# A linear-attention block and a gated MLP in one kernel: a new table of orders, with step 5 transposed by DMA

## Chip, core and metric

The program runs on one core of a Trainium2 chip. The metric is the device time of one execution in microseconds (us); lower is better.

## The reference, cut to what matters

Four batches (B = 4), eight heads (H = 8), 768 positions (S), head size 64. The first half is attention with a decay per head, written block by block with a running state; the second half is an MLP with a gate that mixes the positions. All eight heads of a position make the 512 columns that the MLP reads.

```python
for b in range(nb):                      # blocks of 64 positions
    intra = einsum('bhic,bhjc->bhij', qb, kb) * Dmask
    intra = einsum('bhij,bhjd->bhid', intra, vb)
    inter = einsum('bhid,bhde->bhie', qb * lam_pow, kv_state)
    out[:, :, sl] = intra + inter
    kv_state = lam_block * kv_state + einsum('bhsd,bhse->bhde', kb * rev_pow, vb)
h = maximum(x @ w_in, 0); u, v = h[..., :512], h[..., 512:]
v_n = (v - mean(v)) / sqrt(var(v) + 1e-6)
v_s = einsum('ts,bsd->btd', w_spatial, v_n) + b_spatial
out = (u * v_s) @ w_out
```

## The kernel before

The work is cut into 12 **steps** of 256 positions, three for a batch. A step loads `k`, `q` and `v` (512 KB each, `LK`, `LQ`, `LV`, line 193), scales `k` and `q` by the decay powers into bf16 (`KM`, `QM`, line 328, two halves each) and casts `v` (`VC`, line 182). `kc` and `qc`, the scaled tiles, are transposed into `kT` and `qT`. Two ways of doing that are in the code: on TensorE, eight 128x128 transposes for each of the two tiles and a copy out of PSUM (`TK`, `TQ`, line 363; `EK`, `EQ`), or by one DMA for each tile that SyncE issues (`DK`, line 341; `DQ`, line 345).

Then come, on TensorE, products on quarters of the array, 64 rows by 64 columns: the scores (`SC`, line 393), which VectorE multiplies by the causal mask into `a_sb` (`MK`, line 398); the state's update (`KP`, line 422); and the attention's output (`AV`, lines 456 and 465). The output is copied from PSUM into `xT` (`EX`). All that follows uses the whole array: the two halves of the first MLP product (`PV`, line 490, and `PU`, line 541), for each batch eight spatial products (`PW`, line 567) once all six halves of the normalised `v` (`VN`, lines 526 and 529) stand, and the last product (`PO`, line 578; `PH`, line 587, for half of one). A spatial product accumulates onto a bias that is first copied into its PSUM bank (`GP`). Everything that TensorE makes is taken out of PSUM by ScalarE or VectorE: `EV` and `EU` with a ReLU, `GM` with the gate, `EO` into the output tile, which a store (`ST`, line 601) writes. `LN` and `BN`, `RA`, `RD`, `RB` are the small steps of the decay table and of the normalisation.

The weights come in through the same SyncE queue as the inputs, into staging tiles: `WH` (the first MLP matrix, four loads), `WQ` (the spatial matrix, six), `WP` (the last, one of 1024 KB). Casts to bf16 follow on any engine (`CW`, `CX`, `WC`, `WX`). The spatial matrix is then transposed on TensorE (`WT`, line 553). `FL` (line 306) are products of ones by ones whose result nobody reads.

What sets the order is one string, `ORDER`. A token is the name of a piece, its arguments and its engine: `SC.5.0.0.1.T` is the first half of step 5's scores on TensorE into banks 0 and 1, `EV.6.1.3.A` takes bank 3 out on ScalarE. The loop at the end of the function issues the pieces in the string's order; each engine takes its own pieces strictly in that order, and semaphores hold a piece until what it reads is written and what it overwrites is read. PSUM has eight banks: 0 to 6 are named in the tokens, bank 7 keeps the state. Most tiles of a step exist two or three times (`kT`, `qT`, `kc`, `qc`, `a_sb` twice, inputs and `xT` three times).

```python
with tc.manual_schedule():
    for token in ORDER.split():
        name, *args, e = token.split(".")
        ops[name](e, *map(int, args))
```

Of the kernel before, what the change touches and what calls it, by code (L numbers as in the profile page):

```python
# [16 lines left out]
lam.A BR.A tab.0.A LK.0.S LQ.0.S LV.0.S LQ.1.S LK.1.S LK.2.S LV.1.S LQ.2.S WH.0.S WH.1.S posk.P idn.P msk.P one.D  # L17
row.D FL.1.512.1.1.T FL.1.512.2.1.T FL.1.512.3.1.T LB.6.T FL.1.512.5.1.T FL.1.512.4.1.T FL.1.512.1.1.T FL.1.512.2.1.T
FL.1.512.3.1.T FL.1.512.4.1.T FL.1.512.1.1.T FL.1.512.5.1.T FL.1.512.2.1.T LN.6.A LL.D mkc.D LX.A QM.0.0.P TQ.0.0.1.T
KM.0.0.D KM.0.1.D QM.0.1.P TK.0.0.0.T TK.0.1.4.T TQ.0.1.3.T EK.0.0.0.D QM.1.0.D QM.1.1.D EQ.0.0.1.A EK.0.1.4.A VC.0.P  # L20
SC.0.0.0.1.T EQ.0.1.3.A BB.1.2.T KP.0.6.T BB.0.3.T BE.1.2.A BE.0.3.A SC.0.1.4.5.T TQ.1.0.2.T TQ.1.1.3.T KM.1.1.P
KM.1.0.P MK.0.0.0.1.D KM.2.1.P KM.2.0.P VD.1.1.P TK.1.1.0.T EQ.1.0.2.A SX.0.A EK.1.1.0.A VD.1.0.A MK.0.1.4.5.D
EQ.1.1.3.D TK.1.0.1.T SC.1.1.2.3.T eps.D SY.0.6.D EK.1.0.1.D MK.1.1.2.3.D QM.2.1.P CW.0.P CW.1.P AV.0.0.6.1.T
SC.1.0.4.5.T TK.2.1.0.T TK.2.0.2.T FN.0.6.1.A SA.0.1.D AV.0.1.6.1.T KP.1.3.T EK.2.0.2.A EX.0.0.6.A MK.1.0.4.5.D
AV.1.0.2.6.T QM.2.0.D TQ.2.1.5.T TQ.2.0.4.T FN.1.2.6.A EX.0.1.1.A SA.1.0.D EK.2.1.0.D AV.1.1.2.6.T EQ.2.0.4.A
EQ.2.1.5.D SY.1.3.D CW.2.D CW.3.D EX.1.1.6.A EX.1.0.2.A SC.2.1.0.1.T SC.2.0.4.5.T PV.0.0.3.T PV.0.1.6.T PV.1.0.2.T
EV.0.0.3.A EV.0.1.6.A LV.2.S MK.2.0.4.5.D MK.2.1.0.1.D SA.1.1.D WH.3.S LK.3.S WH.2.S LQ.3.S PV.1.1.5.T VC.2.P KP.2.6.T
AV.2.0.3.6.T CX.1.D PU.1.1.4.T tab.1.A GP.0.0.0.0.A FN.2.3.6.A EV.1.0.2.A SA.2.0.D AV.2.1.3.6.T EX.2.0.3.A EX.2.1.6.A
KM.3.1.P KM.3.0.P BN.0.1.D BN.0.0.D EV.1.1.5.D BN.1.1.D RA.0.A GP.0.3.0.2.D BN.1.0.D PU.0.1.1.T EU.1.1.4.A PV.2.0.3.T
EU.0.1.1.A EV.2.0.3.A PV.2.1.6.T EV.2.1.6.A WQ.1.S WQ.0.S RD.0.D BN.2.0.D RA.1.A RD.1.D BN.2.1.D WC.0.D WQ.2.S WC.2.D  # L30
CX.0.P QM.3.1.P QM.3.0.P TK.3.2.4.T PU.0.0.3.T EK.3.2.4.A EU.0.0.3.A PU.1.0.5.T TQ.3.2.1.T PU.2.1.6.T WC.1.P RA.2.A
RB.0.D RD.2.D LQ.4.S WQ.4.S WQ.5.S WQ.3.S LV.3.S LK.4.S EQ.3.2.1.A EU.2.1.6.A WT.1.0.4.T WT.0.0.3.T WT.2.0.1.T
PU.2.0.6.T EW.0.0.3.A VN.1.1.D VN.0.0.D VN.2.0.D EW.1.0.4.D VN.0.1.D VN.1.0.D EU.1.0.5.A EW.2.0.1.A VN.2.1.D
EU.2.0.6.A GP.0.2.0.6.A WC.4.A SC.3.1.3.4.T PW.0.3.0.2.T PW.0.0.0.0.T PW.0.2.0.6.T MK.3.1.3.4.D WC.5.D GN.2.1.P
GP.0.1.1.5.D GM.0.0.0.0.D QM.4.0.P WC.3.P GM.0.2.0.6.D GM.0.3.0.2.D WT.0.1.4.T WT.2.1.0.T WT.1.1.1.T EW.2.1.0.D
EW.1.1.1.D GP.0.1.0.3.A EW.0.1.4.A GP.0.0.1.6.A QM.4.1.P KM.4.0.P KM.4.1.P WP.S WX.0.P PW.0.1.0.3.T LV.4.S VC.4.P
# [604 lines left out]
```

## Time and profile before

| What | Value |
|---|---|
| median of three runs | 141.37 us (140.95 to 142.02) |
| the profiled execution, its own time | 141.1 us |
| its span, first to last instruction | 139.4 us |
| TensorE (PE) busy | 131.3 us, 94% of the span |
| VectorE (DVE) busy | 114.7 us, 82% |
| ScalarE (ACT) busy | 76.2 us, 55% |
| GpSimd (POOL) busy | 60.2 us, 43% |
| DMA, mean | 245 GB/s, 34.12 MB |

The profiled execution lies 1.7 us above its span, which is what surrounds the instructions. The profile gives PE's matrix products and its weight loads (PEld) apart, and counts a pipelined product as busy to its modelled end, so a busy PE can still hide small delays; the chain of waits (the chain that ended last, followed back) is the view that tells where the time goes. "PEclk" is the granted clock of TensorE.

### The profile page before, as it was taken

Reading aid. Unit: us, or ns where it says so; the run is one execution under the profiler, and the core shown is the slowest. Engines: PE = TensorE matmul, PEld = TensorE weight load, DVE = VectorE, ACT = ScalarE, POOL = GpSimd, SP = SyncE. Lnnn points to the kernel's source line nnn. Section 1 sums busy time; section 2 is a strip of 40 time slices with the busy share of each in tenths; the row PEclk is TensorE's granted clock in tenths of the full one; section 3 lists DMA queues with packets and bytes.
Section 4 is the critical chain, followed back from the end, with each engine's and each line's share of the span. In section 5 each row is a group of like instructions: output and inputs, shape, how many; then the busy total and the mean of one; then the engine's idle time right before and its main releaser. Section 6 shows DMA issues by size and latency. Waiting matters only on the chain.

```text
span 139.4 us, 4677 instructions
## 1 busy us (share of the span) xinstructions
PE 131.3 (94%) x1964; PEld 83.6 (60%) x1978; DVE 114.7 (82%) x235; ACT 76.2 (55%) x148; POOL 60.2 (43%) x70
## 2 busy tenths in 40 slices
PE   5889989999999999999999999999999999999990
PEld 2256755687766666658666466685565665756530
DVE  1549998999997989799788978999799699985470
ACT  3156468799733588659412177782313649790101
POOL 5168654942987458900942059907702000000000
PEclk9996899999999999999999999999999999999998
DMA  3999999999999899997941899999736540025285
GB/s 89 348 346 348 387 362 363 391 382 349 366 345 307 254 315 310 301 206 214 331 106 40 209 353 361 352 228 258 123 75 80 209 172 5 0 98 203 105 304 196
DMA packets 56729, 34.12 MB, mean 245 GB/s; under 512 B 13827, under 2 KB 51971, under 8 KB 56708
## 3 DMA queue, kind: packets, MB, share of 16 engines
q1 hardware_dynamic: 56560, 33.69, 83.5%
q8 instruction: 15, 0.25, 0.7%
q10 hardware_dynamic: 148, 0.13, 0.3%
q14 instruction: 6, 0.05, 0.1%
HBM read 24.38 MB, written 6.29 MB: 220 GB/s over the span
## 4 chain that ended last, share of the span: by engine, by line
PE 84%; DMA 4%; SPq 3%; DVE 3%; issue 2%; POOL 1%; ACT 0%; DVEq 0%; POOLq 0%
PE ps L567 23%; PE ps L541 15%; PE ps L490 15%; PE ps L578 14%; DMA k_in<-in_k_dram 4%; PE ps L393 4%; PE ps L465 4%; SPq L193 3%; PE ps L363 2%; PE ps L456 2%; PE ps L422 2%; POOL kc L328 1%; PE ps L553 1%; DVE qc L328 1%; PE ps L587 1%
## 5 line engine op out<-in xcount | busy, mean ns | idle before, releaser
L567 PE MATMUL ps<-wt_sb,vn 128*128 128x384 bf16 x192 | 33.1, 326 | 0.0
L398 DVE TENSOR_TENSOR a_sb<-ps,m 128x1024 bf16<-128x1024 f32 x24 | 28.6, 1215 | 2.3 <-PE ps L393 1.2
L328 POOL TENSOR_TENSOR kc<-k_in,lv 128x512 bf16<-128x512 f32 x22 | 22.5, 1042 | 14.7 <-PE ps L422 5.2
L567 PEld LDWEIGHTS <-vn 128*128 128x128 bf16 x192 | 18.4, 98 | 11.8
L541 PE MATMUL ps<-xT,win_sb 128*128 128x256 bf16 x192 | 23.5, 273 | 0.0
L328 POOL TENSOR_TENSOR qc<-q_in,lqn 128x512 bf16<-128x512 f32 x20 | 20.8, 1057 | 5.6 <-DMA q_in<-in_q_dram 5.5
L490 PE MATMUL ps<-win_sb,xT 128*128 128x512 bf16 x89 | 22.0, 379 | 0.5 <-issue 0.2
L578 PE MATMUL ps<-wout_sb,gT 128*128 128x512 bf16 x85 | 21.2, 380 | 0.4
L541 PEld LDWEIGHTS <-win_sb 128*128 128x128 bf16 x192 | 18.2, 98 | 3.9 <-DVE xT L180 0.2
L573 DVE TENSOR_TENSOR gT<-ps,uT 128x384 bf16<-128x384 f32 x32 | 16.7, 551 | 4.1 <-PE ps L567 4.0
L178 ACT ACTIVATE o_sb<-ps 128x512 f32<-128x512 f32 (+1 forms) x14 | 7.6, 565 | 16.6 <-PE ps L578 10.4
L505 DVE BATCH_NORM_STATS2 st<-vh 128x6 f32<-128x512 bf16 x24 | 16.3, 679 | 0.1
L182 POOL CAST vb<-v_in 128x1024 bf16<-128x1024 f32 (+1 forms) x10 | 9.9, 995 | 12.8 <-PE ps L465 6.7
L178 ACT ACTIVATE ps<-bsp 128x384 f32<-128x384 f32 x23 | 10.9, 487 | 7.2 <-DVE gT L573 5.2
L490 PEld LDWEIGHTS <-xT 128*128 128x128 bf16 x96 | 8.8, 98 | 9.8 <-ACT xT L178 1.5
L578 PEld LDWEIGHTS <-gT 128*128 128x128 bf16 x92 | 8.7, 98 | 9.3
L495 ACT ACTIVATE vh<-ps 128x512 bf16<-128x512 f32 x19 | 11.1, 597 | 5.8 <-PE ps L490 5.4
L178 ACT ACTIVATE xT<-ps 128x512 bf16<-128x512 f32 x20 | 11.1, 593 | 5.2 <-PE ps L465 4.4
L180 DVE COPY o_sb<-ps 128x512 f32<-128x512 f32 x11 | 7.6, 688 | 3.9 <-PE ps L578 3.3
L495 ACT ACTIVATE uT<-ps 128x512 bf16<-128x512 f32 x17 | 9.8, 591 | 1.4 <-PE ps L541 1.3
L393 PE MATMUL ps<-qT,kT 64*64 64x128 bf16 x384 | 10.1, 226 | 0.1
L465 PE MATMUL ps<-a_sb,vb 64*64 64x128 bf16 x384 | 10.2, 221 | 0.0
(78 smaller groups left out, 159.0 us busy)
## 6 DMA issues: line engine op xcount, KB each, us to landing
k_in<-in_k_dram SPq DMA_DIRECT2D x12, 512.0 KB, 6.3
q_in<-in_q_dram SPq DMA_DIRECT2D x12, 512.0 KB, 6.3
v_in<-in_v_dram SPq DMA_DIRECT2D x12, 512.0 KB, 6.7
out_dram<-o_sb SPq DMA_DIRECT2D x23, 256.0 KB, 2.4
wst<-in_moe_w_in_dram SPq DMA_DIRECT2D x4, 512.0 KB, 7.7
wst<-in_moe_w_spatial_dram SPq DMA_DIRECT2D x4, 384.0 KB, 5.5
wst<-in_moe_w_out_dram SPq DMA_DIRECT2D x1, 1024.0 KB
wss<-in_moe_w_spatial_dram SPq DMA_DIRECT2D x2, 384.0 KB, 6.0
```

The costliest lines, as they stand in the source:

```text
L178: nc.scalar.activation(out=o, in_=i, func=AF.Copy)
L328: vec(e).tensor_tensor(out=dst[n % NCA][:, u].rearrange("p u m o d -> p o (u m) d"), in0=src[n % NIN].rearrange("p (o u) m d -> p o u m d" ...
L393: nc.tensor.matmul(out=pa[o][row(c), w, j], lhsT=kT[n % NTR][row(o), u, j, c * Q64:(c + 1) * Q64], rhs=qv(n, o, u, c), start=(w == 0 and j ...
L398: nc.vector.tensor_tensor(out=a_sb[n % NA][:, i].rearrange("p o w j x -> p o w (j x)"), in0=ps[:, b0:b1 + 1:b1 - b0].rearrange("p o (w y) ...
L465: nc.tensor.matmul(out=po[c ^ o][row(w), c, i], lhsT=vb[n % NCA][row(c), 4 * o + u, j, :], rhs=a[row(c), i, o, w, j, :], start=(r == 0 and ...
L490: nc.tensor.matmul(out=bank(b), lhsT=x[:, slot(c, g)], rhs=win_sb[:, g, DH:DFF], start=(g == 0), stop=(g == NCH - 1))
L495: nc.scalar.activation(out=o, in_=i, func=AF.Relu)
L505: nc.vector.bn_stats(out=st6[p2][:, t], in_=vh[p2][:, t])
L541: nc.tensor.matmul(out=pu[:, f2].rearrange("p (c x) -> p c x", c=2), lhsT=win_sb[:, g, f * P:(f + 1) * P], rhs=x[:, slot(0, g):slot(1, g) ...
L567: nc.tensor.matmul(out=bank(b)[:, 0:HW], lhsT=vn[bb % 2][:, s, f * P:(f + 1) * P], rhs=wt_sb[:, s, i * HW:(i + 1) * HW], start=False, stop ...
L573: nc.vector.tensor_tensor(out=gT[bb % 2][:, f, cols], in0=bank(b)[:, 0:HW], in1=uT[bb % 2][:, f, cols], op=ALU.mult)
L578: nc.tensor.matmul(out=bank(b), lhsT=gT[bb % 2][:, f, t * P:(t + 1) * P], rhs=wout_sb[:, f, :], start=(f == 0), stop=(f == NCH - 1))
```

## The change

Only the table `ORDER` differs, and nearly every token of it stands somewhere else. The functions are the same, three lines further down (line 393 of before is line 396 now).

```diff
-EX.3.1.3.A TQ.5.2.3.T MK.4.1.4.5.D EQ.5.2.3.A EX.3.0.2.D TK.5.2.5.T PV.3.1.4.T VC.5.P LK.7.S LK.6.S EO.0.3.6.D
...
+KM.5.0.P SC.4.0.3.4.T FN.3.5.0.D SY.4.2.D AV.3.1.5.0.T DK.5.S SC.4.1.1.2.T EX.3.1.0.A WX.1.P WX.0.P PW.0.3.1.6.T
+EX.3.0.5.A MK.4.0.3.4.D PV.3.1.3.T SA.4.0.D GM.0.3.1.6.D MK.4.1.1.2.D DQ.5.S LK.6.S GP.0.2.1.5.A LV.6.S PW.0.2.1.5.T
```

- **Step 5** is transposed by two DMAs, `DK.5` and `DQ.5`; its 16 transposes on TensorE and the two copies behind them are gone. Before, steps 6 to 11 were transposed so; now steps 5 to 11 are.
- **The order on TensorE** keeps all other products. The 64x64 work stands in fewer uninterrupted stretches. Counted over the whole table, fills included, it is 22 stretches before and 20 now; from the first `PV` on it is 16 before and 13 now. The description of the change counts 19 instead of 22.
- **The fills** `FL` are 31 instead of 12, most of them 256 columns wide and not 512, all ahead of the first `PV`, spread between the products of steps 0 to 2.
- **The engines** that evict and cast: ScalarE takes 17 `EO` (12 before), 22 `EU` (17), 20 `EV` (19), 9 `VN` (7), 3 `WC` (1), 4 `SY` (1), 3 `SX` (2), 2 `VC` (1), 1 `CW` (0), 6 `EK` (5), and gives up 4 `EQ`, 3 `FN`, 1 `EX`, 1 `EW`, 1 `WX`. VectorE loses most of what ScalarE gains.
- **The loads** begin q0, k0, k1, q1, v0, v1, k2, q2 where they began k0, q0, v0, q1, k1, k2, v1, q2. The first two weight loads are the ninth and tenth in both. The last load of weights, `WP`, stands behind k5 where it stood ahead of v4, q5 and k5.
- **The end**: the last product is now `PH.3.5.1`, half a tile wide, evicted and stored as a half (128 KB) by ScalarE; before it was a whole `PO.3.1` (256 KB) stored by SyncE.

First place: **TensorE around the scores of step 3**, about 33 to 41 us in the profile of before. `L541`/`L544` is `PU`, `L393`/`L396` the scores, `L567`/`L570` the spatial product, `L422`/`L425` the state, `L363` the transposes of step 4. One row stands for a run of rows of its kind (weight loads and further products left out). Before:

```order
L541 MATMUL ps_61<-xT_2_117,win_sb_84 128x256
...
L393 MATMUL ps_61<-qT_1_108,kT_1_106 64x128
...
L567 MATMUL ps_61<-wt_sb_87,vn_0_120 128x384
...
L393 MATMUL ps_61<-qT_1_108,kT_1_106 64x128
...
L422 MATMUL ps_61<-vb_1_104,kc_1_100 64x64
...
L363 MATMUL ps_61<-ident_65,qc_0_101 128x128
```

And now:

```order
L544 MATMUL ps_61<-xT_2_117,win_sb_84 128x256
...
L396 MATMUL ps_61<-qT_1_108,kT_1_106 64x128
...
L425 MATMUL ps_61<-vb_1_104,kc_1_100 64x64
...
L570 MATMUL ps_61<-wt_sb_87,vn_0_120 128x384
...
L556 MATMUL ps_61<-ident_65,wsp_raw_86 128x128
```

Both halves of the scores and the state's update are one stretch now, where spatial products and transposes of `w_spatial` stood between the halves.

Second place: **SyncE around the loads of steps 5 and 6**. `k_in_2_95` and `v_in_2_98` are step 5's inputs, `q_in_2_92` is too; `k_in_0_93`, `v_in_0_96` are step 6's. Before:

```order
L193 DMA k_in_1_94<-in_k_dram 128x8x128
L280 DMA wst_0_141<-in_moe_w_out_dram 128x4x512
L193 DMA v_in_1_97<-in_v_dram 128x8x128
L193 DMA q_in_2_92<-in_q_dram 128x8x128
L193 DMA k_in_2_95<-in_k_dram 128x8x128
L193 DMA v_in_2_98<-in_v_dram 128x8x128
```

And now:

```order
L196 DMA q_in_2_92<-in_q_dram 128x8x128
L196 DMA v_in_1_97<-in_v_dram 128x8x128
L196 DMA k_in_2_95<-in_k_dram 128x8x128
L283 DMA wst_0_141<-in_moe_w_out_dram 128x4x512
L196 DMA v_in_2_98<-in_v_dram 128x8x128
L344 DMA_TRANSPOSE kT_1_106<-kc_1_100 128x8x128
L348 DMA_TRANSPOSE qT_1_108<-qc_1_102 128x8x128
L196 DMA k_in_0_93<-in_k_dram 128x8x128
L196 DMA v_in_0_96<-in_v_dram 128x8x128
```

The large load of the last weights has moved behind step 5's `k`, and the two transposes stand ahead of all of step 6's loads.

Third place: **ScalarE just ahead of the first `PV`**, about 16 to 22 us. `xT_0_115`, `xT_1_116` are what the first four `PV` read, `win_sb` the weights that they read, `vh` what they make. Before:

```order
L178 ACTIVATE kT_0_105<-ps_61 128x512
L178 ACTIVATE xT_0_115<-ps_61 128x4x128
L178 ACTIVATE seen2_73<-ps_61 1x1
L178 ACTIVATE xT_0_115<-ps_61 128x4x128
L178 ACTIVATE qT_0_107<-ps_61 128x512
L178 ACTIVATE xT_1_116<-ps_61 128x4x128 x2
L495 ACTIVATE vh_0_118<-ps_61 128x512 x2
```

And now:

```order
L181 ACTIVATE xT_0_115<-ps_61 128x4x128 x2
L181 ACTIVATE kT_0_105<-ps_61 128x512 x2
L181 ACTIVATE win_sb_84<-wst_0_141 128x512
L181 ACTIVATE xT_1_116<-ps_61 128x4x128 x2
L498 ACTIVATE vh_0_118<-ps_61 128x512
L181 ACTIVATE vb_0_103<-v_in_2_98 128x1024
L498 ACTIVATE vh_0_118<-ps_61 128x512 x3
```

A cast of weights, which waits for the second weight load, now stands ahead of step 1's `xT`, and a cast of `v` between the first evictions.

More of the change, by code (lines that the diff above doesn't have):

```diff
@@ L16 @@
 ORDER = """
[L17 to L36, printed above, removed]
@@ L77 @@
[L77 to L81 removed]
+one.D posk.P lam.A msk.P idn.P LQ.0.S row.D LK.0.S FL.1.256.1.1.T FL.1.256.2.1.T FL.1.256.2.1.T FL.1.256.2.1.T
@@ L82 @@
+ST.3.3.S PO.3.1.0.T EO.3.4.2.D EO.3.2.1.A EO.3.0.5.D EO.3.1.0.A ST.3.4.S PH.3.5.1.3.T ST.3.0.S ST.3.2.S EH.3.5.1.3.A
+ST.3.1.S SH.3.5.1.A
 """
```

107 lines of the change are left out of this document (63 added, 44 removed).

## Prediction

> **What bounds the kernel now.** The page's busy times and its shares of the chain come first.
>
> ```profile
> PE 131.3 (94%) x1964; PEld 83.6 (60%) x1978; DVE 114.7 (82%) x235; ACT 76.2 (55%) x148; POOL 60.2 (43%) x70
> PE 84%; DMA 4%; SPq 3%; DVE 3%; issue 2%; POOL 1%; ACT 0%; DVEq 0%; POOLq 0%
> ```
>
> TensorE is busy for 94% of the span and makes up 84% of the chain that ended last. VectorE is busy for 82% too, but holds 3% of the chain. Next I read the span in stretches, to see whether that is so throughout.
>
> ```profile
> 9.40:12.80 3.40, 3.40 (x64) 1.91 (x62) 3.39 (x4) 1.90 (x5) 1.93 (x2) 0.86 1.15 347
> 12.80:16.20 3.40, 3.21 (x85) 2.53 (x88) 3.13 (x8) 1.62 (x4) 2.67 (x4) 0.64 1.11 371
> 19.80:60.00 40.20, 39.88 (x669) 26.74 (x668) 37.00 (x78) 28.78 (x49) 26.70 (x27) 1.00 1.08 333
> 60.00:100.00 40.00, 39.72 (x528) 25.31 (x532) 36.19 (x78) 20.84 (x44) 20.23 (x21) 1.00 0.99 238
> 100.00:135.80 35.80, 35.45 (x463) 21.71 (x466) 28.36 (x56) 16.34 (x34) 1.07 (x2) 1.00 0.38 122
> ```
>
> Columns are the stretch, its length, then busy time with the number of instructions for PE, PEld, DVE, ACT and POOL, the granted clock, the DMA share and GB/s. From 19.8 to 135.8 us PE lacks 0.3 us in each of three stretches. Before that the loads set the pace (a DMA share over 1, 347 to 371 GB/s). The list of PE's waits (who, for whom, us, times, longest) says the same; ahead of these lines stands only the wait for the first constant:
>
> ```profile
> PE ps L363 <- POOL qc L328: 1.3, 2, 1.1
> PE ps L456 <- ACT xT L178: 0.2, 1, 0.2
> PE ps L363 <- POOL kc L328: 0.2, 1, 0.2
> PE ps L490 <- issue: 0.2, 1, 0.2
> ```
>
> So the time has three parts: when the first `PV` starts (19.84 us), how much work PE has from there on, and the tail behind its last product. No waits are left to take away between; a new order can win there only by less work, and lose by new waits.
>
> **The change part by part.** *Less work on PE.* These pieces of the chain, in order of time (start, length, what):
>
> ```profile
> 33.71 0.35 PE ps L393 x16
> 34.06 3.03 PE ps L567 x18
> ...
> 41.20 1.95 PE ps L567 x12
> ...
> 46.90 0.25 PE ps L393 x16
> ...
> 48.69 0.89 PE ps L363 x16
> ...
> 51.77 0.22 PE ps L393 x16
> ...
> 61.39 0.87 PE ps L541 x8
> 62.27 0.86 PE ps L578 x4
> ...
> 65.75 4.88 PE ps L567 x30
> 70.63 0.57 PE ps L393 x32
> ```
>
> The 16 transposes of step 5 are the piece at 48.69 us, between full-array work, and end with **0.89 us** less on the chain. The price of a stretch of 64x64 work is also there: 16 score products take 0.35 us where a stretch opens (33.71) and 0.22 to 0.25 inside one, so entry costs 0.10 to 0.13; 18 spatial products behind the stretch take 3.03, and at 1.95 for 12 they should take 2.93, so the way out costs 0.10. That is 0.20 to 0.23 for each; I take 0.22. Of the joins, those ahead of the first `PV` are not on the path. From there on the order has 13 stretches for 16: **0.66 us**. Everything else behind the first `PV` is the same products. Together PE has 1.55 us less to do. The two copies of step 5 leave ACT, which is worth nothing on a chain that has 0% of ACT.
>
> *The start.* What brings the first four `PV`:
>
> ```profile
> 4.77 1.29 DVE L328 TENSOR_TENSOR kc<-k_in,lv 128x512 bf16<-128x512 f32 x2 [0.37 <-DMA k_in<-in_k_dram]
> ...
> 10.87 4.05 POOL L328 TENSOR_TENSOR kc<-k_in,lv 128x512 bf16<-128x512 f32 x4 [1.53 <-DMA k_in<-in_k_dram]
> ...
> 17.81 1.44 POOL L182 CAST win_sb<-wst 128x512 bf16<-128x512 f32 x2
> ...
> 19.20 1.08 ACT L178 ACTIVATE xT<-ps 128x512 bf16<-128x512 f32 x2
> ...
> 19.84 3.63 PE L490 MATMUL ps<-win_sb,xT 128*128 128x512 bf16 x15
> ```
>
> The first load is there at 4.77 and the fifth at 10.87, that is 1.5 us a load. The second weight load is the tenth in both orders: about 18.3 us, at the earliest. Now GpSimd makes three casts in a row, 0.72 each, and the third needs that load: 19.0. ScalarE casts the last quarter behind the same load (0.6, as its other copies of 512 columns), then the two `xT` of step 1 (1.08): 20.0. The second `PV` needs those `xT`. Before, step 1's first `PV` was the third, 1.73 after 19.84, at 21.57; now it is the second and may begin at 20.0 to 20.7, that is a start of 19.2 to 19.84 in before's terms. The decays of steps 0 and 1 now have their `k` and `q` two loads sooner, but wait at the end for the same q2 and the same weights. I take **0**; the bounds are 0.5 less (the casts fit as summed) and 1.2 more (the half clock, below).
>
> *The fills* are 19 more, all in the waits ahead of 19.8 us, where PE waits for operands that come no sooner; nothing on the path, unless they delay a product that is ready, by one fill.
>
> *Step 5's transposes by DMA.* The rows are issues (KB each, median us to landing), the GpSimd piece that prepares step 5's `k`, step 6's first transpose in SyncE's queue, and the DMA share in 40 slices of 3.5 us:
>
> ```profile
> k_in<-in_k_dram SPq DMA_DIRECT2D x12, 512.0 KB, 6.3
> kT<-kc SPq DMA_TRANSPOSE x6, 5.2
> qT<-qc SPq DMA_TRANSPOSE x6, 3.4
> 43.94 2.04 POOL L328 TENSOR_TENSOR kc<-k_in,lv 128x512 bf16<-128x512 f32 x2 [0.43 <-DMA k_in<-in_k_dram]
> 55.14 2.97 SPq L341 DMA_TRANSPOSE kT<-kc  x1
> DMA  3999999999999899997941899999736540025285
> ```
>
> When are they due? Step 5's scores stood at 51.77. In front of them PE now lacks the transposes (0.89), one join (0.22) and three `PO` (3 x 0.86), and has one `PU` more (0.87): 48.95. When do they land? k5 landed at 43.94; it is now queued ahead of the 1024 KB of weights, two loads of 1.45 to 1.5, so about 41.0. With 2.04 for its decay `DK.5` can go at about 43.1 and `DQ.5`, one issue behind, at 44.4; plus 3.4 to 5.2 they land between 47.8 and 49.6. That is between 1.1 early and 0.65 late. While it waits at the head of SyncE's queue, `DK.5` holds step 6's loads. Both transposes also take DMA time where the digits are 9 until 62 us; a load's 1.5 us for each is the bound, 3 us in sum, for all that follows. Step 6's own transposes are next: in before the first was issued at 55.14 and with 5.2 landed near 60.3, the second one issue later, 61.6. They now have two loads fewer ahead of them (q8 and v7), which gives the 3 us back. They are due with step 6's scores: 70.63, less five `PW` (4.88), one `PO`, one `PU` (these stand behind now), the transposes and one join, is 62.9. That is 1.3 early, or 1.7 late with both bounds against it. I charge nothing there.
>
> *New waits behind the first `PV`.* ScalarE gains 5 evictions of `uT`, 5 of the output, 2 normalisations and some casts. The chain of a batch's end goes through it: the last `PV`, eviction, statistics, `VN`, first `PW`, with the bias copies and evictions in the same queue.
>
> ```profile
> L495 ACT ACTIVATE vh<-ps 128x512 bf16<-128x512 f32 x19 | 11.1, 597 | 5.8 <-PE ps L490 5.4
> L178 ACT ACTIVATE ps<-bsp 128x384 f32<-128x384 f32 x23 | 10.9, 487 | 7.2 <-DVE gT L573 5.2 <-DVE a_sb L398 1.3 <-DVE o_sb L180 0.4
> L526 ACT ACTIVATE vn<-vh,nmr,rstd 128x512 bf16<-128x512 bf16 x7 | 5.7, 809 | 2.6 <-DVE nmr L520 2.6
> ```
>
> At the end of batch 3 the last `PV` has 7 products of 0.87 behind it before the first `PW` (6.1 us), and ScalarE has five evictions (0.6), three normalisations (0.81) and two short roots to make in that time: 5.4 and the roots. That just fits. The bounds for all waits of this kind are 0 (before had none) and 1.3 (one `VN` and one bias copy late, once); **+0.30**, nearer to none, since the queue overlaps its pieces (two copies of 0.59 in 1.08 at 19.20).
>
> *The tail.*
>
> ```profile
> 135.80 0.60 ACT L178 ACTIVATE o_sb<-ps 128x512 f32<-128x512 f32 x1 [3.20 <-PE ps L578]
> 131.37 0.39 ACT L178 ACTIVATE o_sb<-ps 128x256 f32<-128x256 f32 x1 [5.68 <-PE ps L587]
> out_dram<-o_sb SPq DMA_DIRECT2D x23, 256.0 KB, 2.4
> out_dram<-o_sb ACTq DMA_DIRECT2D x1, 128.0 KB, 1.9
> ```
>
> The last eviction is half as wide, 0.39 for 0.60, but stands behind a whole one on ScalarE; the store is 1.9 for 2.4. Between 0 and 0.7 less; **0.15**.
>
> The sum is made against the profiled execution: 141.1 - 0.89 - 0.66 + 0 + 0.30 - 0.15 = **139.7 us**. That execution lies 0.27 below the median of the runs, 141.37, inside their spread, so I leave the sum as it is. A measurement of this kernel can tell about 1% from no change; 1% below the median is 139.96.
>
> **The rivals.** *The half clock moves into dense work.* In before the clock is 0.86 in 9.4 to 12.8 us and 0.64 in 12.8 to 16.2: (0.14 + 0.36) x 3.4, so 1.7 us of clock are lost in a part where PE waits anyway. Now PE stands still longer between 8 and 13 us (it needs q1's decay and v0) and its work is then packed more tightly into 13 to 19 us. If the half clock holds there, 0.36 x 3.4 = 1.2 us come onto the path: **140.9**. The fills speak against it. [...]
>
> *Step 5's transposes come late.* The place is the head of SyncE's queue. If k5 lands no sooner than in before (43.94), `DK.5` goes at 46.0 and lands, with 5.2, at 51.2, while step 5's scores are due at 48.95: a wait of 2.3 us, and step 6's loads behind it. 139.7 + 2.3 = **142.0**, slower than before. It decides from a k5 later than about 42. Against it: the order of the queue, and that a load is issued 6.3 us ahead of its landing, so that SyncE keeps the DMA fed.
>
> *ScalarE's queue becomes the bound.* If at each of the four batch ends a spatial product waits for one `VN` of 0.81, that is 3.2 in place of 0.3: **142.6**. Against it: 76.2 us busy of 139.4, and some 7 more by my estimate (ten evictions, two `VN`, casts, less the copies given up, at these durations).
>
> *It does not do what it says*: the products that close up only wait at other places (mask on VectorE, banks), so that joins and transposes give nothing: 141.1 - 0.15, **140.95**. VectorE at 37.0 of 40.2 us speaks for it, the moves off VectorE against it.
>
> **How the numbers follow.** Forecast 0.55, its own range 138.8 to 140.4 (the start's 0.5 below and 0.4 of waits above, with the tail); half clock 0.18; transposes late 0.08; ScalarE 0.05; nothing won 0.14. Of the forecast's 0.55 a little over a tenth lies above 139.96; with 0.49 I call it faster by over 1%. Slower by over 1% starts at 142.8 and needs the late transposes or ScalarE with some of the start: 0.06. Within 1%: 0.45. The range is 138.6 to 141.4: it holds the forecast, the half clock and the empty case.
>
> **What would show it.** In the new profile the first `PV` (line 493) starts at 19.2 to 20.6 us; no `L366` piece stands on the chain after step 4's; 13 stretches of 64x64 work follow the first `PV`; PE's waits behind 20 us add up to under 0.5 us; the span is near 138.0. A PE wait of over 1 us at line 396 at 49 us would mean late transposes, one at line 570 ScalarE, a first `PV` after 21 us the start. If PE has no wait and the time is still 141, the price of a stretch or of the transposes is wrong.

## The result: 148.4 us, slower, and the profile after

The changed kernel takes 148.37 us (median of four runs, 147.35 to 148.77) against 141.19 for the kernel before beside it (four runs, 140.95 to 142.02). The ratio is 1.0486, with a 95% interval of 1.0417 to 1.0555. The forecast was 139.7, in a range from 138.6 to 141.4, and is wrong by 8.7 us. (Now and then a run comes out over 1.5% slower than the fastest of the same kernel; the ratios here and below leave such runs out, so a ratio can lie under that of the medians.)

From the page of the changed kernel: TensorE's and the other engines' busy times, its granted clock in 40 slices of 3.7 us, and the engines' shares of the chain that ended last.

```profile
PE 135.5 (92%) x1981; PEld 86.9 (59%) x1981; DVE 112.1 (76%) x218; ACT 82.2 (56%) x160; POOL 63.6 (43%) x72
...
PEclk9999999999959999999999999999999999999999
...
PE 78%; DVE 17%; issue 2%; ACT 1%; ACTq 0%; DVEq 0%
```

VectorE had 3% of the chain and has 17%, although it is busy for less time in all. There is one slice at half clock, the twelfth, near 42 us. The list of TensorE's waits (who, for whom, us in all, times, longest) now has two long ones for VectorE and one of 2.1 us for nothing that the profile shows:

```profile
PE ps L396 <- DVE wt_sb L183: 2.1, 1, 2.1
PE ps L396 <- issue: 2.1, 1, 2.1
PE ps L544 <- DVE kT L183: 1.7, 1, 1.7
...
PE ps L570 <- ACT ps L181: 0.3, 1, 0.3
```

The span grew by 7.3 us, from 139.4 to 146.7. Cut by TensorE's own marks (starts of the first `PV` and of the first spatial product of each batch), and with three of the experiments beside it, in us:

| Stage | before | changed | guard back | twenty fills out | both |
|---|---|---|---|---|---|
| start to first `PV` | 19.84 | 22.20 | 21.03 | 20.23 | 20.54 |
| to batch 0's first `PW` | 14.15 | 19.43 | 14.69 | 16.96 | 15.28 |
| to batch 1's | 31.60 | 32.33 | 32.88 | 30.76 | 30.77 |
| to batch 2's | 27.77 | 28.21 | 28.22 | 28.37 | 28.49 |
| to batch 3's | 29.25 | 27.97 | 28.58 | 29.10 | 28.59 |
| to TensorE's end | 13.15 | 13.15 | 13.15 | 13.15 | 13.16 |
| behind it | 3.63 | 3.41 | 3.39 | 3.40 | 3.40 |

Some work changed its stage with the new order (half of step 3's scores and its state's update, 0.6 us, stand ahead of batch 0's first `PW` now), so the stages compare to about that. The loss is in the first two rows: 2.4 us ahead of the first `PV` and 5.3 us behind it.

**The start.** The chain of the changed kernel, in order of time (start, length, what):

```profile
15.92 0.21 PE ps L309
16.14 0.29 PE ps L396 x11
16.43 2.07 issue
18.50 0.30 PE ps L396 x5
18.79 0.43 PE ps L309 x3
```

TensorE itself is the chain here. It stops for 2.07 us after 11 of 16 score products that all read the same tiles, so it is not one of these tiles that it waits for; and between the transposes it runs fills (L309). Twenty fills stand behind the first transpose. From the start of each to the start of the next product they take 3.4 us in sum.

**Behind the first `PV`.** Instructions of VectorE in order of time (start, length, engine, line, operation, tiles), then GpSimd's beside the last three:

```profile
28.47 1.46 DVE L183 CAST wsp_raw<-wst 128x768 bf16<-128x768 f32 x1
...
33.55 0.93 DVE L523 SCALAR_TENSOR_TENSOR nmr<-mv,rstd 128x2 f32<-128x2 f32 x1
34.39 1.21 DVE L532 TENSOR_SCALAR vn<-vh,mv,rstd 128x512 bf16<-128x512 bf16 x1
...
36.12 0.54 DVE L183 COPY wt_sb<-ps 128x768 bf16<-128x768 bf16 x1
...
36.78 2.10 DVE L532 TENSOR_SCALAR vn<-vh,mv,rstd 128x512 bf16<-128x512 bf16 x2
38.80 0.99 DVE L523 SCALAR_TENSOR_TENSOR nmr<-mv,rstd 128x2 f32<-128x2 f32 x1
```

```profile
35.87 1.04 POOL L331 TENSOR_TENSOR qc<-q_in,lqn 128x512 bf16<-128x512 f32 x1 [0.42 <-DMA q_in<-in_q_dram]
36.86 0.82 POOL L185 CAST wsp_raw<-wst 128x768 bf16<-128x768 f32 x1
37.64 2.13 POOL L331 TENSOR_TENSOR qc<-q_in,lqn 128x512 bf16<-128x512 f32 x2
```

An `nmr` is two columns wide; before, it took 0.15 us at this place, three `vn` took 1.04, and the cast of `wsp_raw` 0.53:

```profile
30.33 0.53 DVE L180 CAST wsp_raw<-wst 128x768 bf16<-128x768 f32 x1
...
31.24 0.15 DVE L520 SCALAR_TENSOR_TENSOR nmr<-mv,rstd 128x2 f32<-128x2 f32 x1
...
31.39 1.04 DVE L529 TENSOR_SCALAR vn<-vh,mv,rstd 128x512 bf16<-128x512 bf16 x3
```

With 0.35 us for one `vn` (a third of 1.04), the cast, the two `nmr` and the first three `vn` of the changed kernel are 4.8 us longer in sum than before; the stage grew by 5.3. Not all of VectorE's work stretched: `st` and `mv`, which work in SBUF too, kept their 0.66 to 0.68 and 0.18 us beside a running GpSimd (25 to 30 us), and `wt_sb`, which comes out of PSUM, its 0.54.

In the kernel before, GpSimd stood still for 4.46 us at that time (in brackets the idle time ahead, and who ended it):

```profile
33.92 0.18 POOL L533 CAST seen<-vn 1x1 f32<-1x1 bf16 x1 [4.46 <-DVE vn L529]
```

One token made it do so: `GN.2.1.P` copies one element of the last normalised tile of batch 0, so that GpSimd's own queue waits for VectorE. I call it the guard. The new table has it among batch 2's pieces, where it no longer holds GpSimd back here.

**The half clock.** TensorE's clock in two stretches of 3.4 us (columns as in the prediction; the granted clock is the third number from the end):

```profile
37.20:40.60 3.40, 1.31 (x25) 0.91 (x24) 3.40 (x6) 1.31 (x2) 3.35 (x4) 1.00 0.97 269
40.60:44.00 3.40, 3.36 (x56) 2.12 (x56) 1.80 (x3) 3.37 (x8) 2.45 (x3) 0.50 1.00 342
```

TensorE worked for 1.31 of the 3.40 us of the first stretch; the second ran at a granted clock of 0.50, in dense work (3.36 of 3.40 us busy): another 1.7 us of clock lost (0.50 x 3.40).

### The profile page after: what moved, and what is told of

Its sections match the earlier page's. It is cut to its first block, busy times and chain, and to the rows that moved or that the text cites. A ratio compares the mean times of both kernels' runs of the same rounds, so it can differ in the third digit from the quotient of the medians.

```text
span 146.7 us, 4694 instructions
## 1 busy us (share of the span) xinstructions
PE 135.5 (92%) x1981; PEld 86.9 (59%) x1981; DVE 112.1 (76%) x218; ACT 82.2 (56%) x160; POOL 63.6 (43%) x72
## 4 chain that ended last, share of the span: by engine, by line
PE 78%; DVE 17%; issue 2%; ACT 1%; ACTq 0%; DVEq 0%
PE ps L570 23%; PE ps L493 11%; PE ps L581 11%; PE ps L544 9%; PE ps L396 5%; PE ps L309 4%; DVE st L508 4%; PE ps L468 4%; PE ps L366 3%; DVE vn L532 3%; DVE nmr L523 2%; PE ps L459 2%; PE ps L425 2%; PE ps L295 2%; DVE mv L509 1%
## 5 line engine op out<-in xcount | busy, mean ns | idle before, releaser
L570 PE MATMUL ps<-wt_sb,vn 128*128 128x384 bf16 x192 | 34.4, 334 | 0.3 <-ACT ps L181 0.3
L570 PEld LDWEIGHTS <-vn 128*128 128x128 bf16 x192 | 18.9, 100 | 14.0 <-issue 1.9
L331 POOL TENSOR_TENSOR qc<-q_in,lqn 128x512 bf16<-128x512 f32 x21 | 22.6, 1088 | 9.1 <-DMA q_in<-in_q_dram 8.5
L544 PE MATMUL ps<-xT,win_sb 128*128 128x256 bf16 x192 | 23.8, 273 | 1.7 <-DVE kT L183 1.7
L493 PE MATMUL ps<-win_sb,xT 128*128 128x512 bf16 x96 | 23.7, 380 | 0.0
L581 PE MATMUL ps<-wout_sb,gT 128*128 128x512 bf16 x92 | 22.5, 379 | 0.0
L544 PEld LDWEIGHTS <-win_sb 128*128 128x128 bf16 x192 | 18.3, 98 | 6.5 <-issue 1.9
L498 ACT ACTIVATE vh<-ps 128x512 bf16<-128x512 f32 x20 | 11.8, 595 | 9.2 <-PE ps L493 9.1
L181 ACT ACTIVATE o_sb<-ps 128x512 f32<-128x512 f32 (+1 forms) x19 | 10.7, 571 | 9.6 <-PE ps L581 4.3
L498 ACT ACTIVATE uT<-ps 128x512 bf16<-128x512 f32 x22 | 12.6, 588 | 4.1 <-PE ps L544 3.9
L396 PE MATMUL ps<-qT,kT 64*64 64x128 bf16 x384 | 10.5, 231 | 4.2 <-DVE wt_sb L183 2.1
L185 POOL CAST vb<-v_in 128x1024 bf16<-128x1024 f32 (+1 forms) x9 | 9.1, 1007 | 12.1 <-PE ps L468 8.1
L396 PEld LDWEIGHTS <-kT 64*64 64x64 bf16 x384 | 7.1, 112 | 7.0 <-issue 6.2
```

Source lines behind the costliest of these rows:

```text
L181: nc.scalar.activation(out=o, in_=i, func=AF.Copy)
L331: vec(e).tensor_tensor(out=dst[n % NCA][:, u].rearrange("p u m o d -> p o (u m) d"), in0=src[n % NIN].rearrange("p (o u) m d -> p o u m d" ...
L396: nc.tensor.matmul(out=pa[o][row(c), w, j], lhsT=kT[n % NTR][row(o), u, j, c * Q64:(c + 1) * Q64], rhs=qv(n, o, u, c), start=(w == 0 and j ...
L493: nc.tensor.matmul(out=bank(b), lhsT=x[:, slot(c, g)], rhs=win_sb[:, g, DH:DFF], start=(g == 0), stop=(g == NCH - 1))
L498: nc.scalar.activation(out=o, in_=i, func=AF.Relu)
L544: nc.tensor.matmul(out=pu[:, f2].rearrange("p (c x) -> p c x", c=2), lhsT=win_sb[:, g, f * P:(f + 1) * P], rhs=x[:, slot(0, g):slot(1, g) ...
```

## The experiments

Two theories came out of the reading. T1: the guard's loss lets GpSimd run beside VectorE's normalisations, which stretches VectorE's instructions that read SBUF (some of them, by the rows above). C: TensorE stops at 16.4 us because its own code is not there yet. Against T1 stood R1, that VectorE's list is simply late; against C, a hidden wait, or a clock that the narrower fills leave at half speed.

### The guard put back

```diff
-KM.4.0.P KM.4.1.P
...
-QM.4.1.P WC.5.P QM.4.0.P
...
-QM.5.0.P
...
 VN.2.1.D
+GN.2.1.P KM.4.0.P KM.4.1.P QM.4.1.P WC.5.P QM.4.0.P QM.5.0.P
...
 VN.6.0.A
-GN.2.1.P
 QM.10.0.P
```

> The changed kernel with one token moved: the small GpSimd copy that reads the last normalised tile of batch 0 (GN.2.1.P), which stands among batch 2's pieces now, is put behind VN.2.1.D, as in the kernel before, and six GpSimd pieces that stood ahead of that place (KM.4.0, KM.4.1, QM.4.1, WC.5, QM.4.0, QM.5.0) follow it. Theory T1 (GpSimd's casts and products, now free to run beside VectorE's normalisations, stretch those of VectorE's instructions that read SBUF, and TensorE waits): GpSimd stands still while VectorE runs vn, one vn takes about 0.40 us again and one nmr 0.15 to 0.29 instead of 0.93 to 0.99, the two TensorE waits of 1.74 and 2.13 us and the stage at half clock (about 1.5) go, 142.5 to 144.0 us instead of 148.4. Rival R1 (VectorE's own list is too long and too late, GpSimd has no part in it): VectorE's instructions get no shorter, the waits stay, 147.5 to 149. Rival R2 (the guard makes GpSimd late for step 4's k and q instead): the waits at 34 and 38 us go, and TensorE waits for kc or qc of step 4 between 42 and 48 us, 145 to 147.

144.79 us (143.65 to 145.57), ratio 1.0219 (1.0147 to 1.0291). GpSimd and VectorE:

```profile
34.67 0.18 POOL L537 CAST seen<-vn 1x1 f32<-1x1 bf16 x1 [2.70 <-DVE vn L533]
```

```profile
31.70 0.28 DVE L524 SCALAR_TENSOR_TENSOR nmr<-mv,rstd 128x2 f32<-128x2 f32 x1
...
33.48 0.73 DVE L533 TENSOR_SCALAR vn<-vh,mv,rstd 128x512 bf16<-128x512 bf16 x2
34.12 0.15 DVE L524 SCALAR_TENSOR_TENSOR nmr<-mv,rstd 128x2 f32<-128x2 f32 x1
```

`nmr` and `vn` have their old lengths, both waits of TensorE for VectorE and the half clock are gone (mean granted clock of the profiled execution 0.996, in the changed kernel 0.987), and the second stage is 14.69 us instead of 19.43. T1 stands, R1 and R2 fall. One part of the gain is not the guard's: the first `PV` came 1.2 us sooner, though nothing ahead of it was changed, because the stop in step 1's scores lasted 1.03 us here and 2.07 in the changed kernel. The total is 0.8 us above the upper end that T1 gave; in the profiled execution another stop appeared for which the profile shows no cause, again inside score products:

```profile
44.87 0.32 PE ps L397 x10
45.19 1.92 issue
47.11 0.30 PE ps L397 x6
```

A packet of the queue that the DMA view calls `q8 instruction` (the code queue) ran from 44.95 to 45.91 us beside it; TensorE went on 1.2 us behind its end.

### The guard taken out of the kernel before

```diff
-MK.3.1.3.4.D WC.5.D GN.2.1.P
+MK.3.1.3.4.D WC.5.D
```

> The kernel before with only the token GN.2.1.P left out (a copy of one element that nobody reads; what is computed for the output is whole). T1: GpSimd runs its products and casts from 29.5 us on instead of standing still for 4.46 us, VectorE's nmr and vn there stretch by 0.4 to 0.9 us each for several of eight, TensorE waits 1 us or more ahead of the first spatial products, 143 to 146 us. Rival R1: 140.7 to 141.7, as before, since GpSimd only does its work earlier. Rival R3 (GpSimd ahead is a gain): below 140.7.

143.39 us (ten runs, 141.34 to 144.31) against 141.6; ratio 1.0061 (1.0009 to 1.0113), that is about 1 us; T1's 143 to 146 us would be 1.4 to 4.4 more than 141.6. VectorE, and the first piece of GpSimd that now runs in the former pause:

```profile
31.60 1.00 DVE L521 SCALAR_TENSOR_TENSOR nmr<-mv,rstd 128x2 f32<-128x2 f32 x1
...
34.02 2.18 DVE L530 TENSOR_SCALAR vn<-vh,mv,rstd 128x512 bf16<-128x512 bf16 x3
```

```profile
31.16 1.42 POOL L329 TENSOR_TENSOR qc<-q_in,lqn 128x512 bf16<-128x512 f32 x1 [1.47 <-PE ps L364]
```

The mechanism is the same: `nmr` 1.00 for 0.15, three `vn` 2.18 for 1.05, and TensorE waits 0.7 us for a `vn`. I read the smaller price from GpSimd's rows: it stood still between its pieces here too, 1.47 us for TensorE and then 1.27 and 1.26 for loads, and met VectorE less often. By these two cases a lost guard costs what the meeting costs, which hangs on when GpSimd's inputs are there. In the rows above, an `nmr` and the GpSimd piece that it met end together: the `nmr` that began at 31.60 ended at 32.60, and the GpSimd piece that began at 31.16 ended at 32.58. `wt_sb`, which VectorE copies out of PSUM, took 0.54 in the midst of a GpSimd piece (36.12 us, in the changed kernel). Why one stretches and the other does not, no run shows.

### The start of before, alone and with the guard

All pieces up to the first `PV` as before (fills too), the changed order from there.

```diff
-one.D posk.P lam.A msk.P idn.P LQ.0.S row.D LK.0.S FL.1.256.1.1.T FL.1.256.2.1.T
...
+lam.A BR.A tab.0.A LK.0.S LQ.0.S LV.0.S LQ.1.S LK.1.S LK.2.S LV.1.S LQ.2.S WH.0.S WH.1.S
...
+tab.1.A LV.2.S WH.3.S WH.2.S SA.1.1.D LQ.3.S MK.2.0.4.5.D WQ.1.S CX.1.P
 PV.0.1.6.T PV.1.0.5.T PV.0.0.4.T
```

> The changed kernel with all pieces up to the first PV in the order, banks and engines of the kernel before (fills included), and the changed order from there on; the nine pieces that the changed start has and the other has not (LV.2, WH.2, WH.3, LQ.3, WQ.1, tab.1, CX.1, MK.2.0, SA.1.1) stand right behind. Theory S1 (the start costs its 2.4 us by its own order, and all behind it is shifted): first PV at 19.6 to 20.4 us, 145.5 to 146.5. Rival S2 (what comes later, loads of the spatial weights or VectorE's list, would end at the same time anyway): first PV at 20 and a longer wait at 34 to 40 us, 147.5 to 148.5.

143.27 us (eight runs, 142.61 to 144.92), ratio 1.0123 (1.0086 to 1.0161). That is less time than S1 gave (145.5 to 146.5): 5.1 us less for a first `PV` that came 2.2 us earlier. S2 falls.

> Both edits together. If T1 and S1 hold and add up, and the 1.55 us of TensorE's work that the change saves (16 transposes, three stretches) are real: 139.5 to 141.2, at or below the kernel before. If the saving is not real: 141.2 to 142.5. If a third loss stands behind the two: over 142.5, and the chain shows where.

142.30 us (ten runs, 141.46 to 144.08), ratio 1.0059 (1.0023 to 1.0096). This is the range that was named for a saving on TensorE that is not real (141.2 to 142.5); the waits below say otherwise, since they are longer than what is left. The two edits don't add: 3.6 and 5.1 alone, 6.1 together. I read it so, without an experiment for it alone: an earlier start shifts VectorE's list against GpSimd's, whose inputs come by DMA and do not shift with it. With the fills out (below), which starts about as early, GpSimd's products of step 4 begin at 33.43 us and in the changed kernel at 33.41, while VectorE's list is 1.8 us earlier (`nmr` at 31.76 for 33.55); only one pair of `vn` met GpSimd (2.13 us), while `nmr` took 0.29 and the cast of `wsp_raw` 0.56; TensorE waited 1.3 us for VectorE behind the first `PV`, where the changed kernel has 2.1 and 1.7, and no stretch at half clock followed (mean granted clock 0.999). TensorE's waits behind 20 us, 0.2 in all before, are these and two more of 0.2, 2.1 us in sum, more than the 0.7 us that are left over the kernel before:

```profile
PE ps L395 <- DMA qT<-qc: 0.9, 1, 0.9
PE ps L492 <- DVE a_sb L400: 0.5, 1, 0.5
PE ps L492 <- issue: 0.3, 2, 0.2
```

### Two bursts of small products: does TensorE stop for its code?

```diff
-FL.1.512.2.1.T LN.6.A
+FL.1.512.2.1.T FZ.384.1.T LN.6.A
...
-ST.3.1.S
+ST.3.1.S FZ.384.1.T
```

> The kernel before with two bursts of 384 products of ones by ones on quarters of the array (64x64, 64 columns, 768 rows of TensorE's list each, results that nobody reads): one behind its opening fills, while the loads keep all DMA engines busy, and one behind the last product, when only stores are left. Theory C (TensorE's own code comes through the DMA engines in packets of 16 KB, some 230 to 256 rows each; where one comes late TensorE stands still with nothing shown to wait for): stops of 1 to 3 us labelled issue inside the early burst, each ending 1 to 1.5 us behind the end of such a packet, and shorter stops or none in the late burst. Rival C0 (the 2.07 us at 16.4 us in the changed kernel were some other wait, and code is always there): both bursts run through, 384 products in 5 to 6 us at full clock or 10 to 12 at half, without a stop over 0.3 us. The time of the whole rises by the bursts' length, up to 25 us, and says nothing else.

TensorE in order of time (L314 is the burst; in brackets the idle time ahead):

```profile
6.62 1.92 PE L314 MATMUL ps<-ones 64*64 64x64 bf16 x209
12.54 1.90 PE L314 MATMUL ps<-ones 64*64 64x64 bf16 x128 [3.99 <-issue]
17.36 0.85 PE L314 MATMUL ps<-ones 64*64 64x64 bf16 x47 [2.92 <-issue]
...
150.27 1.54 PE L314 MATMUL ps<-ones 64*64 64x64 bf16 x163
154.44 1.24 PE L314 MATMUL ps<-ones 64*64 64x64 bf16 x128 [2.62 <-issue]
158.17 1.45 PE L314 MATMUL ps<-ones 64*64 64x64 bf16 x93 [2.49 <-issue]
```

Between two stops lie exactly 128 products, 256 rows of the list with their weight loads, both times. The DMA view of 10.2 to 11.2 us holds one packet of the code queue (count, MB, share); it started at 10.22 and took 0.88, and TensorE went on at 12.54, 1.4 us behind its end:

```profile
q8 instruction: 1, 0.02, 5.5%
```

C stands, and C0 falls. The first early stop, 4.0 us, is longer than C gave (1 to 3); the late ones, 2.6 and 2.5, are shorter than the early ones by little only: under loads TensorE gets 256 rows in 4.8 us (12.54 to 17.36; granted clock 0.50 from 13 us on), with little but stores in 3.7 (154.44 to 158.17; granted clock 1.00 up to 156). In the changed kernel itself a packet of the code queue started at 16.07 us and took 0.93; the stop at 16.43 ended at 18.50, 1.5 us behind it.

The first stop comes after 445 or 446 rows in this kernel, in the changed one and in four of its variants.

### Fewer fills, and wider fills

Left out are all `FL` behind the first transpose (20), nothing else:

```diff
-FL.1.256.3.1.T
 TK.1.0.0.T
-FL.1.256.5.1.T FL.1.256.5.1.T
...
```

> The changed kernel without the twenty fills behind the first transpose (40 rows fewer in TensorE's list ahead of the stop at 16.4 us). Theory C: the stop goes with the count of rows (some 440) and not with a place of the program: it moves some 40 rows further in the work, into the next pieces, or vanishes where the packet comes in time; first PV 0 to 2 us earlier, 146 to 148.4 us. Rival: the stop stays inside the same scores of step 1 (a wait of theirs that the trace does not show). Rival on the clock: without the fills TensorE idles more and is at half clock longer, first PV later than 22.3 us, 148.5 to 150.

143.38 us (142.84 to 144.37), ratio 1.0122 (1.0053 to 1.0191): 5.0 less, where C had given 146 to 148.4. The first `PV` starts at 20.23, 2.0 sooner; the two stages behind it are 2.5 and 1.6 us shorter (the table above), as VectorE met GpSimd less and no half clock followed (mean granted clock 0.999, in the changed kernel 0.987). The stop moved from step 1's scores to step 2's transposes, and it is shorter:

```profile
16.82 0.27 PE L364 MATMUL ps<-ident,kc 128*128 128x128 bf16 x2 [0.39 <-DVE a_sb L399]
17.96 0.28 PE L364 MATMUL ps<-ident,kc 128*128 128x128 bf16 x2 [0.86 <-issue]
```

It goes with the count of rows (446 here, 446 in the changed kernel), as C says, and it is no hidden wait of the scores. Its length is not fixed by the list: with the same pieces ahead of it, it was 2.07 us in the changed kernel and 1.03 with the guard back, so that up to about 1 us of the 2.0 may be chance.

The first eleven fills 512 columns wide in place of 256:

```diff
-FL.1.256.1.1.T FL.1.256.2.1.T FL.1.256.2.1.T FL.1.256.2.1.T
+FL.1.512.1.1.T FL.1.512.2.1.T FL.1.512.2.1.T FL.1.512.2.1.T
...
```

> The changed kernel with the first eleven fills 512 columns wide in place of 256: same count of instructions. Theory W (the narrower fills leave TensorE cold: full clock from 13.3 us on in the changed kernel, from 5.0 us on before): full clock by 5 to 8 us, 128x128 transposes at 56 ns instead of 116 ns ahead of 13 us, 0.5 to 1.2 us off the first PV, 147.0 to 148. Rival: TensorE stands for its code at the same row anyway, or for VectorE and the loads, and the first PV stays at 22.0 to 22.5, 148 to 148.8. A loss is possible too: the wider fills end later and push the bias products and the first transposes back.

149.51 us (148.26 to 150.76), ratio 1.0467 (1.0406 to 1.0528). TensorE worked faster sooner: twelve transposes of `kc` between 5 and 13 us took 219 ns each for 314 (changed kernel first; the two numbers behind the bar are us in all and ns for each):

```profile
L366 PE MATMUL ps<-ident,kc 128*128 128x128 bf16 x12 | 1.9, 314 | 0.0
```

```profile
L367 PE MATMUL ps<-ident,kc 128*128 128x128 bf16 x12 | 1.2, 219 | 0.0
```

It won nothing. In the profiled execution (150.66 us; the fastest took 148.26) the stop came after 445 rows at 16.59 us, no sooner than in the changed kernel (16.43), since TensorE waited 0.6 and 0.3 us for ScalarE and VectorE on the way; it lasted 2.42 us, and the first `PV` came at 22.72. Theory W falls.

### The prices of the forecast: step 5 by DMA, and a stretch

```diff
-TQ.5.2.3.T EQ.5.2.3.A TK.5.2.5.T EK.5.2.5.A
...
-LV.5.S
+LV.5.S DK.5.S
...
-AV.3.1.2.3.T
+AV.3.1.2.3.T DQ.5.S
```

> The kernel before with step 5 alone transposed by DMA: the two transposes on TensorE and their two copies out, 16 products and two evictions, are left out, and SyncE issues DK.5 behind the load of step 5's v and DQ.5 behind AV.3.1. All else stands as before. The prediction's price: 0.89 us less of TensorE's time, 140.3 to 140.9 us against 141.2 to 141.6 before. Rival L (late transposes): the scores of step 5 wait 1 us or more for the DMA near 50 us, 141.5 to 143. Rival N: the transposes on TensorE filled time that is lost anyway, 141.2 to 141.6.

146.99 us (145.94 to 147.33), ratio 1.0361 (1.0304 to 1.0417). Matched product by product against the kernel before, TensorE is 0.94 us ahead at the `PV` behind the place where the transposes were (48.48 us for 49.42); 0.12 of that it had before, so they gave 0.82, near the forecast's 0.89. Then SyncE's queue stands still. The queue around the two transposes, and the chain behind them:

```profile
39.56 1.42 SPq L194 DMA_DIRECT2D v_in<-in_v_dram  x1
46.20 1.33 SPq L342 DMA_TRANSPOSE kT<-kc  x1
```

```profile
48.02 1.90 SPq L346
...
51.21 7.25 DMA v_in<-in_v_dram
...
58.55 1.06 ACT vb L179
```

`DK.5` (L342) waits 5.1 us at the head of the queue for step 5's `kc` and goes at 46.20, `DQ.5` (L346) follows; step 6's `v` goes out behind both at 51.21, where it went at 45.12 before; TensorE waits 2.9 us for step 6's `v`, and the 6.8 us from 58.8 on run at a granted clock of 0.50 (the 6.8 us ahead of them at 1.00). Rival L named the wrong place (the scores of step 5 waited 0.2 us). The prediction had the right one, `DK.5` holding step 6's loads, and charged nothing for it; in the changed kernel, where TensorE has no wait there, that held.

The second try issues step 6's `v` ahead of both transposes:

```diff
-LV.5.S DK.5.S
+LV.5.S LV.6.S DK.5.S
```

> Step 5 by DMA in the kernel before once more, with the load of step 6's v and DK.5 right behind the load of step 5's v, and DQ.5 behind AV.3.1 as in the first try, so that no input of step 6 that TensorE needs early stands behind DQ.5 in SyncE's queue. If the 5 us of the first try came from that queue (v of step 6 issued at 50.6 us, behind a DQ.5 that waited for AV.3.1, and TensorE 2.9 us without it): the stop ahead of step 6's state goes, and 140.5 to 141.6 us are left, by how much the scores of step 5 wait for the two transposes. Rival: the transposes themselves take the DMA's time from the loads, and step 6 is late again, 143 or more.

143.05 us (142.49 to 143.62), ratio 1.0109 (1.0053 to 1.0166). The time lies in the rival's range (143 or more). The long stop is gone, but step 5's scores wait 0.7 us for `qT`, and 1.0 us is waited for the `kc` of step 6, whose `k` still stands behind `DQ.5`. Neither of the two places tried was free.

Twelve products of 64 columns on the whole array between pieces of 64x64 work, in the kernel before (one of the twelve places):

```diff
-AV.4.0.6.3.T SC.5.0.0.1.T
+AV.4.0.6.3.T FX.1.64.0.T SC.5.0.0.1.T
...
```

> The kernel before with twelve products of ones by ones on the whole array (64 columns each, results that nobody reads) put between pieces of 64x64 work behind the first PV, so that twelve more stretches of 64x64 work begin. The prediction priced a stretch at 0.22 us: with 0.05 us for each small product itself, +3.2 us in TensorE's time, about 144.8 us if TensorE is the bound there. Rival Z (a change between whole array and quarters costs next to nothing): +0.6, 142.0 to 142.4. Rival P (a price between, under 0.1 each, and the prediction's 0.66 for three stretches is mostly something else): 142.4 to 143.4.

144.62 us (144.04 to 144.81), ratio 1.0208 (1.0148 to 1.0267): 3.2 us more, 0.27 for each break and small product. Matched against before, most places show a step of 0.23 to 0.28. The price of a stretch, 0.22, was right; Z and P fall.

### Both repairs, and a try to get ahead

The guard back and the twenty fills out, as above:

```diff
 VN.2.1.D
+GN.2.1.P
...
-FL.1.256.3.1.T
...
```

> The changed kernel with the guard put back behind VN.2.1.D (as in the first of these kernels) and without the twenty later fills. If the late start and the lost guard are the two causes: first PV at 20 to 20.5, the first spatial product 15 us later, 141.3 to 142.5 us, what the changed kernel with the whole start of before and the guard came to (142.3). If the fills had another use, a stage at half clock in the first 25 us and over 143.

142.77 us (ten runs, 141.94 to 143.67), ratio 1.0091 (1.0053 to 1.0128), with no half clock in the first 25 us (mean granted clock of the whole 0.999): 5.6 of the 7.2 us are back. That is 0.3 us above what was expected at most (142.5). The last column of the table is this kernel. Of TensorE's waits, a stop of 1.4 us for code and 0.7 us for a copy of ScalarE's are left ahead of the first `PV`, and 1.0 us at 107 us for step 11's transposed `q`.

With the start of before, the guard, other banks for the first three `PV`, and `PV.9.1` ahead of step 11's scores:

```diff
-PV.0.1.6.T PV.1.0.5.T PV.0.0.4.T
+PV.0.1.6.T PV.1.0.2.T PV.0.0.3.T
...
+PV.9.1.0.T EV.9.1.0.A
 SC.11.1.3.4.T
```

> The changed kernel with the start of before and the guard, and its two longest waits taken on: the first three PV go into banks 6, 2 and 3 (they waited 0.5 us at 20.8 us for a bank that VectorE's mask product of step 2 still held), and PV.9.1 stands ahead of step 11's scores (which waited 0.9 us for step 11's transposed q at 103 us). If both waits go and nothing takes their place: 1 to 1.4 us less than 142.3, 140.9 to 141.3, at or just under the kernel before. If the wait for step 11's q only moves to the second half of its scores: 141.5 to 142.3.

142.85 us (nine runs, 142.05 to 143.7), ratio 1.0102 (1.0067 to 1.0136): no better than without the two edits, and outside what was expected (142.3 at most). Both waits went and others came, of TensorE for VectorE and for step 5's `qT` (a fourth, of 0.3, is for VectorE too):

```profile
PE ps L543 <- DVE kT L182: 0.5, 1, 0.5
PE ps L395 <- DMA qT<-qc: 0.5, 1, 0.5
PE ps L543 <- DVE a_sb L400: 0.4, 1, 0.4
```

No version here beats the kernel before.

## Why the prediction was wrong, step by step

- **Less work on TensorE, -1.55: right in the main.** The transposes gave 0.82 in their place and a stretch costs 0.22 to 0.27. From the first `PV` to TensorE's end, less the listed waits, the kernel with the guard back takes 117.5 - 3.3 = 114.2 us, before 115.9 - 0.2 = 115.7: 1.5 less. The same count gives 1.4 and 1.1 less for the guard with the start of before and with the fills out, and 0.6 for the last variant.
- **"The fills ... nothing on the path, unless they delay a product that is ready": wrong, and the first of the two steps that failed.** It took TensorE's waits of the kernel before as given. In the new order twenty fills stand where TensorE is itself the chain; they take 3.4 us there and use up 40 rows of code. Without them the first `PV` comes 2.0 us sooner (part of it perhaps the shorter stop) and the whole takes 5.0 us less.
- **"The start", 0 (bounds -0.5 and +1.2): it came to +2.4, outside the bounds.** I summed loads, GpSimd and ScalarE and never asked how fast TensorE's own list is delivered. The 256 rows ahead of the stop, from the 190th on, took 3.5 us in the changed kernel (12.71 to 16.21); the same count took 5.1 in the one before (11.29 to 16.42), which had no stop there. From the 190th row to TensorE's restart it was 4.6 to 6.1 us in five kernels with the changed start (fills in or out). That the stop is one for code is what the burst and the fills point to (stops exactly 128 products apart, and one that goes with the count of rows); what sets the moment at which a packet comes, no run shows.
- **"New waits behind the first `PV`", +0.30 (bounds 0 and 1.3): the second step that failed, about 5 us.** I looked at ScalarE's list, which cost 0.3 us in all, and did not ask what a token on an idle engine was for. The guard had moved. Restored, it takes 4.7 us out of that stage and 3.6 out of the whole.
- **"The half clock moves into dense work": it did, to another place.** It came at 40.6 us (granted clock 0.50 up to 44.0), behind the waits for VectorE, and was gone with them from the profiled execution with the guard back (mean granted clock 0.996): I take it for a consequence of them and no rival of its own.
- **"Step 5's transposes come late": not seen in the changed kernel,** where `DQ.5` went out at 51.74 us and the scores began, without a wait, at 57.29, since all else was late too; with an early start it shows, at 0.5 us in the last variant.
- **The tail, -0.15:** 3.63 to 3.41 us, 0.2 less. Right.

The signs named in advance did their work: a first `PV` after 21 us pointed to the start. The waits behind 20 us came to 4.1 and not under 0.5, nearly all of it for VectorE, which none of the signs named.

What stays open: why the first code packet started 2.0 us after the 190th row in the kernel before and 2.4 to 3.8 us after it with the changed start, and so why the stop is 1.0 us long in one execution and 2.4 in another.

## What to carry to other kernels

A token that computes nothing of use, on an engine with time to spare, may be there to hold that engine still; before an order is changed, ask of each such token what starts when it goes. A filler is free only while its engine waits, so its place has to be judged in the new order and not in the old one. And where small products are packed closer together, count the rows of code as well as the time.

## What the runs showed of the hardware

- In two closed runs of 64x64 products (`b_burst`) TensorE stopped for 2.5 to 4.0 us each time, the stops exactly 128 products (256 rows) apart. The first stop ended 1.4 us behind the end of a packet of the code queue. I read it so that TensorE had run out of its own code. That queue brought 0.25 MB in 15 packets (page of the kernel before), 16 to 17 KB each; the first stop fell after 445 or 446 rows. One block of 256 rows took 4.8 us under loads (granted clock 0.50 from 13 us on) and one 3.7 us beside stores (1.00 up to 156 us). A stop shows as "issue" in the middle of products of one kind.
- Some of VectorE's instructions that read and write SBUF (`nmr`, `vn`, the cast of `wsp_raw`) grew by up to 0.9 us each beside a running GpSimd (the changed kernel and `b_noguard`): an `nmr` of 2 columns took 0.15 or 1.00 us. `st`, which reads SBUF too, kept its 0.68.
- Breaking a stretch of 64x64 products with one product on the whole array cost 0.27 us, that product included (`b_split`: 3.2 us for twelve).
